# Sliding-window attention with a mixture of experts: values loaded twice per query block, one product per block and pair of heads

## The chip, the cores and the metric

The kernel runs on one core of a Trainium2 chip. Its engines are TensorE (PE, matrix products; PEld is its loading of weights), VectorE (DVE), ScalarE (ACT), GpSimd (POOL) and SyncE (SP, which here only issues DMAs). The metric is the device time of one execution in microseconds (us); the median of several runs counts.

## The reference

```
def _attn_ref(q, k, v):                       # 8 batches, 8 heads, 576 tokens, head size 64, float32
    scores = scale * np.matmul(q, k.transpose(0, 1, 3, 2))
    rel = pos[:, None] - pos[None, :]
    mask_plain = (rel >= 0) & (rel < 32)                          # heads 0 to 3
    mask_dil = (rel >= 0) & (rel < 32 * 4) & (rel % 4 == 0)       # heads 4 to 7
    scores = np.where(masks, scores, -1e9); attn = softmax(scores)
    return np.matmul(attn, v)

def _moe_ref(x, w_gate, w1, w2, capacity):    # x: 4608 x 512, 8 experts, capacity 80, hidden 1024
    probs = softmax(x @ w_gate); expert = argmax; gate_w = probs[expert]
    for e in range(8):
        tok = the (at most 80) tokens of expert e with the largest gate_w
        out[tok] = gate_w[tok] * (np.maximum(x[tok] @ w1[e], 0) @ w2[e])
    return out                                # rows of all other tokens are zero
```

## The kernel before

**Layout.** The dilated heads' tokens are permuted on the host, so that in both kinds of heads a block of 32 queries needs at most 64 keys: its own block of 32 and the block before it. `plan` puts four query blocks of 32 (one for each quarter of the 128 partitions) and both halves of the heads into one *tile*; there are 36 tiles, 4.5 for each of the 8 batches. In a tile `a` counts four pairs of heads (two plain, two dilated) and `u` the head within a pair. Keys (`k2`) and values (`v4`) of the two heads of a pair stand on alternate partitions, with zeros in the other head's place, so that one product serves both heads.

**A tile's chain** (`tile_chain`, L909): `scores` (L391) adds the mask through an identity product (L396, four of them) and multiplies queries and keys (L403, 16 products of 128 columns; each float32 product makes two rows in the trace). `smax` (L408) and `ssub` (L412) run on DVE, `sexp` (L418) on ACT. `ptrans` (L422) transposes the probabilities on PE, four products. `pcopy` (L428) brings them from PSUM into the tile `pts`: two copies of 64 partitions on ACT for one parity of key blocks, one of 64 partitions on DVE for the other. `pts` has a slot for a key block as a query block's own and one as the block before it; what isn't written stays zero from the start (L361). `pv` (L437) multiplies by the values: each value block of 64 keys stands in `v4` once, so a query block with an even number needs two products (its own block and the one before lie in different spans) and one with an odd number one product; a tile has mostly 24. `raw` (L459, ACT) copies the result out, `norm_r` (DVE) and `norm` (L469, POOL) divide by the sum, the row goes to DRAM (`xs`, L975), `xtrans` (L474) transposes it on PE, and `xcopy` (L498, ACT) puts pieces of it into `xT`.

**Gate and ranks.** For each batch `gate`, `fields`, `counts` and `merge` choose the 80 best tokens for each expert, in small steps on all engines beside the tiles. After the last tile they end in the list `irow` (L1048), from which `gather` (L284, an indirect DMA of POOL) fetches the tokens of the first expert.

**Experts.** Each expert has eight weight chunks of 512 KB (`wr`, `load_wc`, L166). `wsplit` (L181) splits one into a high part (`wh`, ACT, L191) and a low part (`wl`, DVE or POOL, L193), and `g1` and `g2` (L1079, L1111) run three products for each pair of parts. Of 64 chunks 11 are loaded during the tiles (L880, from tile 8 on every second tile), four at the last tile (L953), the rest when buffers come free.

**Order of work.** A planner (`drive`, L218) fixes the order of instructions on PE, DVE, ACT and POOL ahead of time from durations and penalties in the constants L32 to L41. Everything on the SP queue stands in the order of the calls: after tile i's scores a load of queries for tiles i+3 and i+4 (`after_scores`), after its row has gone out values (`after_norm`, L900) and every third time 512 KB of zeros for the output (`zero_out`, L386); the eight that are left go out after the last tile. A DMA on this queue waits until the one eight places ahead of it has landed. `warm` (L324) issues PE products whose results nobody reads: 40 at the start (`W0`), 15 at tile 2 (`W1`), 30 after the lists are ready (`W2`), and groups of eight between the last ranking steps (`NWA`, 88 in all).

Of the kernel before, what the change touches and what calls it, by code (L numbers as in the profile page):

```python
# [23 lines left out]
DIL = 4  # L24
# [11 lines left out]
d_sc, d_pv, d_ex = 1.25, 1.5, 0.55  # L36

l_pe, lat, LA, AGE = -0.011, 0.147, 5, 0.162
p_sc, p_pt, p_pv, p_xt, p_bg, e_bg, e_ct, e_mg, e_fl = -0.204, 0.096, 0.389, 0.407, 0.345, -0.051, 0.341, 0.278, 0.59
e_split, e_splitd, p_split, p_splitd, p_splitp, q_hi, q_lo, q_lop = 2.997, 0.642, 0.764, -0.636, 2.782, 1.204, 1.134, -1.508  # L40
q_ga, q_in, p_wa, q_h, q_hp, d_x, p_mg, p_fl = -2.51, 0.414, 0.723, 0.74, 0.248, 0.0, 0.332, 1.008  # L41


def plan(B, S):


    nb = S // 32
    lin = [(b, j) for b in range(B) for j in range(nb)]
    q = [[lin[4 * t:4 * t + 4], lin[4 * t:4 * t + 4]] for t in range(len(lin) // 4)]
    v = [[list(h) for h in t] for t in q]  # L50
    if B % 2 == 0 and nb == 18:
        o = [0, 9, 4, 13, 2, 1, 10, 5, 14, 11, 6, 15, 16, 7, 8, 3, 12, 17]
        w = [0, 1, 8, 9, 12, 13, 4, 5, 2, 3, 10, 11, 14, 15, 6, 7, 16, 17]
        b, t0 = B - 1, len(q) - 5
        for lst, od in ((q, o), (v, w)):
            seq = lst[t0][1][:2] + [(b, j) for j in od]
            for k in range(5):
                lst[t0 + k][1] = seq[4 * k:4 * k + 4]
    for t in q:

        t[1] = [t[1][i] for i in (1, 0, 3, 2)]
    return q, v
# [7 lines left out]
def build_consts(B, S, E, C):  # L70
    NC = -(-S // P)
    ncc = B * NC
    q, _ = plan(B, S)
    bf = ml_dtypes.bfloat16
    masks, sig, held = [], [], {}
    for halves in q:
        m = np.zeros((P, 2, 64), np.float32)
        for h in range(2):
            for n, (b, j) in enumerate(halves[h]):
                qi = 32 * j + np.arange(32)[:, None]  # L80

                ki = 32 * j + (np.arange(64) - 32 if j % 2 else np.arange(64) % 32 - 32 * (np.arange(64) // 32))[None, :]
# [37 lines left out]
def moe_attn_kernel(ctx: ExitStack, tc: tile.TileContext, io, dims, sig):  # L120
# [9 lines left out]
    KW = NG * S  # L130
    HB = S // 2
# [3 lines left out]
    qplan, vplan = plan(B, S)  # L135
    vpos = {}
    for t, halves in enumerate(vplan):
        for h in range(2):
            for i, bk in enumerate(halves[h]):
                assert bk[1] % 2 == i % 2  # L140
                vpos[h, bk] = (t, i // 2)
# [76 lines left out]
    def drive(chains, cost, done):  # L218
# [7 lines left out]
        while not done():  # L226
# [6 lines left out]
            for c in chains:  # L233
                ask = c[1]() if callable(c[1]) else c[1]
                if ask is not None:
                    eng, d, r = ask
                    s0 = max(clock[eng.split(".")[0]], r + l_pe * (eng[:2] == "PE"))
                    k = s0 + cost(c, eng, s0)
# [3 lines left out]
            _, end, c, eng, d = best  # L242
            clock[eng.split(".")[0]] = end
            advance(c, end)

# [14 lines left out]
    def split_lo(name):  # L260
# [5 lines left out]
        def ask():  # L266
            for (e, c, p, n), r in mine():
                return name, (0.00225 if pool_ else 0.00113) * 1024 / n + 0.03, r
# [25 lines left out]
    with ExitStack() as c2:  # L294
# [10 lines left out]
        NV = 3  # L305
# [29 lines left out]
        k2 = [qp.tile([P, 2, KW + HB], F32, name=f"k2_{i}") for i in range(2)]  # L335
# [4 lines left out]
        pts = [kp.tile([P, 2, 2, 2, 2, 2, 32], F32, name=f"pts_{i}") for i in range(2)]  # L340
# [7 lines left out]
        KS = (0, 64, 160, HB)  # L348
        kv = [k[:, :, 0:KW].rearrange("p u (a x) -> p u a x", a=2 * NG) for k in k2]
        nc.vector.memset(zero, 0.0)  # L350
        for u in range(2):
            nc.vector.memset(kv[0][:, u, :, 0:KS[1]], 0.0)
        for i in (1, 2):
            for u in range(2):
                (nc.vector, nc.gpsimd)[u].memset(kv[0][:, u, :, KS[i]:KS[i + 1]], 0.0)
# [4 lines left out]
        for i in range(2):  # L360
            nc.vector.memset(pts[i], 0.0)  # L361
        for u in range(2):
            nc.gpsimd.memset(k2[1][:, u, 0:KW], 0.0)
# [914 lines left out]
```

## Time and profile before

| | before |
|---|---|
| median of 3 runs | 327.98 us (325.33 to 331.28) |
| profiled execution, its own time | 326.13 us |
| its span, first to last instruction | 324.3 us |
| PE busy in the span | 291.6 us, 90% |
| DVE, ACT, POOL busy | 235.6, 196.7, 163.2 us |
| moved by DMA | 85.11 MB, 262 GB/s over the span |
| granted TensorE clock, mean | 0.974 of full speed |

The profile's page gives busy time by engine, the span in 40 slices (PEclk is the TensorE clock that was granted, in tenths), the chain of work that ended last, and the costliest groups of instructions with what ended the idle time before them. "issue" is time in which an engine waited for nothing that the profile shows. The stages are: up to 19 us the first loads; to 195 us the tiles; to 214 us the last ranks; from 216 us the experts; the span ends at 324.3 us.

### The profile page before, as it was taken

Reading aid. Unit: us, or ns where it says so; the run is one execution under the profiler, and the core shown is the slowest. Engines: PE = TensorE matmul, PEld = TensorE weight load, DVE = VectorE, ACT = ScalarE, POOL = GpSimd, SP = SyncE. Lnnn points to the kernel's source line nnn. Section 1 sums busy time; section 2 is a strip of 40 time slices with the busy share of each in tenths; the row PEclk is TensorE's granted clock in tenths of the full one; section 3 lists DMA queues with packets and bytes.
Section 4 is the critical chain, followed back from the end, with each engine's and each line's share of the span. In section 5 each row is a group of like instructions: output and inputs, shape, how many; then the busy total and the mean of one; then the engine's idle time right before and its main releaser. Section 6 shows DMA issues by size and latency. Waiting matters only on the chain.

```text
span 324.3 us, 11403 instructions
## 1 busy us (share of the span) xinstructions
PE 291.6 (90%) x4615; PEld 221.0 (68%) x4615; DVE 235.6 (73%) x636; ACT 196.7 (61%) x519; POOL 163.2 (50%) x208
## 2 busy tenths in 40 slices
PE   7669999999897999997999998778999999999992
PEld 6448788778776778766778875654566666666661
DVE  6327757969756868867879788785997887887550
ACT  6106567464743655762664763473889889889560
POOL 9302225356644833152333353359978878655522
PEclk9959999999999999999999999995999999999997
DMA  5973989949995889986734528977959999998000
GB/s 145 304 298 101 331 300 365 408 148 330 346 346 191 236 293 342 346 316 205 259 105 166 197 71 284 403 249 247 357 186 321 379 396 379 390 380 314 20 20 21
DMA packets 31396, 85.11 MB, mean 262 GB/s; under 512 B 5744, under 2 KB 7408, under 8 KB 30448
## 3 DMA queue, kind: packets, MB, share of 16 engines
q1 hardware_dynamic: 30064, 81.76, 70.9%
q0 software_dynamic: 1280, 2.62, 2.6%
q8 instruction: 36, 0.59, 0.8%
q14 instruction: 16, 0.13, 0.1%
HBM read 64.19 MB, written 20.19 MB: 260 GB/s over the span
## 4 chain that ended last, share of the span: by engine, by line
PE 50%; DMA 15%; DVE 14%; issue 8%; ACT 7%; POOL 3%; SPq 1%; POOLq 0%; ACTq 0%; DVEq 0%
PE pv L454 10%; PE sc L403 8%; PE hp L1087 7%; PE yps L1119 7%; PE xt L478 4%; PE pT L426 4%; DMA wr<-in_w 4%; DMA out<-zero 3%; DVE wl L193 3%; DMA k<-in_k 3%; PE sc L396 3%; DMA xs<-x 2%; DVE pts L434 2%; ACT wh L191 2%; ACT xT L503 2%
## 5 line engine op out<-in xcount | busy, mean ns | idle before, releaser
L193 DVE TENSOR_TENSOR wl<-wr,wh 128x1024 fp32r<-128x1024 f32 (+1 forms) x54 | 70.5, 1349 | 12.1 <-ACT wh L191 11.9
L471 POOL TENSOR_TENSOR x<-xr,rc 128x512 f32<-128x512 f32 x35 | 36.9, 1055 | 78.2 <-DVE rc L467 33.8
L191 ACT CAST wh<-wr 128x1024 fp32r<-128x1024 f32 (+1 forms) x72 | 64.0, 954 | 1.0 <-PE yps L1119 0.5
L454 PE MATMUL pv<-v,pts 128*32 128x130 f32 x1664 | 56.6, 274 | 4.1 <-issue 4.1
L454 PEld LDWEIGHTS pv<-v,pts 128*32 128x32 f32 x1664 | 47.0, 108 | 7.7 <-issue 7.0
L403 PE MATMUL sc<-k,q 128*32 128x128 f32 x1152 | 42.8, 289 | 6.2 <-DMA k<-in_k 3.5
L193 POOL TENSOR_TENSOR wl<-wr,wh 128x1024 fp32r<-128x1024 f32 (+1 forms) x18 | 41.0, 2282 | 14.4 <-PE yps L1119 7.5
L403 PEld LDWEIGHTS sc<-k,q 128*32 128x32 f32 x1152 | 35.5, 116 | 11.3 <-issue 8.1
L462 ACT COPY xr<-pv 128x520 f32<-128x520 f32 x35 | 20.7, 591 | 36.1 <-PE pv L454 35.3
L503 ACT COPY xT<-xt 128x64 f32<-128x64 f32 (+3 forms) x195 | 33.6, 312 | 13.1 <-PE xt L478 12.8
L434 DVE COPY pts<-pT 64x512 f32<-64x512 f32 x36 | 25.0, 694 | 19.3 <-ACT pts L432 18.8
L410 DVE TENSOR_REDUCE mx<-sc 128x8 f32<-128x512 f32 x36 | 24.6, 684 | 11.3 <-PE sc L403 10.8
L432 ACT COPY pts<-pT 64x256 f32<-64x256 f32 x72 | 23.7, 381 | 12.3 <-PE pT L426 12.2
L420 ACT ACTIVATE ex<-ex 128x512 f32<-128x512 f32 x36 | 23.0, 638 | 12.1 <-DVE ex L415 11.7
L415 DVE TENSOR_TENSOR ex<-sc,mx 128x512 f32<-128x512 f32 x36 | 24.8, 689 | 4.7 <-PE pT L426 3.8
L1087 PE MATMUL hp<-wh,xh 128*80 128x512 f32 x64 | 26.6, 416 | 0.4 <-ACT xh L1077 0.4
L287 POOL DMA_INDIRECT xg<-xs,irow x16 | 23.1, 1444 | 6.9 <-issue 3.4
L1087 PE MATMUL hp<-wl,xh 128*80 128x512 f32 x64 | 26.2, 410 | 0.2 <-DVE wl L193 0.2
L1087 PE MATMUL hp<-wh,xl 128*80 128x512 f32 x64 | 26.2, 409 | 0.0
L1119 PE MATMUL yps<-wh,hh 128*80 128x512 f32 x64 | 25.3, 395 | 0.0
L1119 PE MATMUL yps<-wh,hlo 128*80 128x512 f32 x64 | 25.2, 394 | 0.1
L1119 PE MATMUL yps<-wl,hh 128*80 128x512 f32 x64 | 25.0, 391 | 0.0
(137 smaller groups left out, 509.4 us busy)
## 6 DMA issues: line engine op xcount, KB each, us to landing
wr<-in_w SPq DMA_DIRECT2D x64, 512.0 KB, 7.6
v<-in_v SPq DMA_DIRECT2D x36, 260.0 KB, 4.2
xs<-x SPq DMA_DIRECT2D x36, 256.0 KB, 4.0
out<-zero SPq DMA_DIRECT2D x18, 512.0 KB, 6.6
q<-in_q SPq DMA_DIRECT2D x17, 512.0 KB, 6.9
k<-in_k SPq DMA_DIRECT2D x14, 576.0 KB, 6.2
q<-in_q SPq DMA_DIRECT2D x2, 256.0 KB, 3.0
k<-in_k SPq DMA_DIRECT2D x2, 256.0 KB, 7.8
```

The lines of the kernel that those rows point to most:

```text
L191: nc.scalar.copy(hi[:, s], w[:, s])
L193: eng.tensor_tensor(out=lo[:, s], in0=w[:, s], in1=hi[:, s].bitcast(F32), op=ALU.subtract)
L403: nc.tensor.matmul(out=ps[32 * j:32 * j + 32, a], lhsT=q[:, a // 2, a % 2, j, :], rhs=k2[b % 2][:, :, o:o + 2 * w].rearrange("p u (r y) -> ...
L410: nc.vector.tensor_reduce(out=st[t]["mx"], in_=st[t]["sc"].rearrange("p a u r k -> p (a u) (r k)"), axis=AX.X, op=ALU.max)
L415: nc.vector.tensor_tensor(out=st[t]["ex"].rearrange("p a k u -> p a u k"), in0=st[t].pop("sc").rearrange("p a u r k -> p a u (r k)"), in1= ...
L432: nc.scalar.copy(pts[t % 2][0:64, h, :, :, h], ps[0:64, h])
L434: nc.vector.tensor_copy(out=pts[t % 2][64:P].rearrange("p h g e s i q -> p (h g) (e s) i q")[:, :, 1:3], in_=ps[64:P].rearrange("p h g e i ...
L454: nc.tensor.matmul(out=ps[32 * j:32 * j + 32, h, 2 * g * (D + 1):2 * (g + 1) * (D + 1)].rearrange("p (u d) -> p u d", u=2), lhsT=pts[t % 2 ...
L471: eng.tensor_tensor(out=st[t]["x"].rearrange("p (h a) d -> p h a d", h=2), in0=st[t][of][:, :, :, 0:D], in1=st[t]["rc"].unsqueeze(3).broad ...
L503: copy(out=dst, in_=ps[:, HC * hh:HC * hh + HC, col:col + n])
L1087: nc.tensor.matmul(out=fs[e]["hp"][n][0:C], lhsT=a_[:, c, :], rhs=b_[:, sl], start=(c == 0 and q == 0), stop=(c == NKC - 1 and q == 2))
L1119: nc.tensor.matmul(out=fs[e]["y"][0:C], lhsT=a_[:, f, :], rhs=b_[:, sl], start=(f == 0 and q == 0), stop=(f == NFC - 1 and q == 2))
```

## The change

The values' layout in DRAM now holds, for each query block, the 64 keys from the block before it to its own end, so every value stands there twice. `load_v` loads one tile at a time, 2 x 260 KB, into four buffers (`NV`; before: two tiles at a time into three). `pv` is one product for each query block and pair of heads, 16 in a tile, with no accumulation. `pcopy` is one copy of all 128 partitions into a tile from a pool, on ACT or DVE, as the planner finds (`either`): 23 on ACT and 13 on DVE. `pts` isn't zeroed any more. Keys have a row of their own for each pair of heads with 32 zeros ahead, and are loaded in three pieces of 128, 192 and 256 keys. The dilated blocks of a tile aren't swapped, so a tile's `xT` is copied in fewer pieces (116 on ACT; before 195 on ACT and two on DVE). The first queries go through ACT's queue. Zeros go out after every sixth tile, and 13 of the 18 after the last. The four weight chunks of the last tile are requested behind its row. The planner's constants are others; it adds a price where PE goes from products of 32 columns to whole ones. `W2` is 64 and `NWA` is 0.

```diff
-ZR, ZI, IW, W0, W1, W2, XC, SP0 = 2, 6, 8, 40, 15, 30, 1, 2
-FB, CB, TE, NWA, XC0 = 3, 6, 34, 8, 2
-CUTS = (2,)
+ZR, ZI, IW, W0, W1, W2, XC, SP0 = 2, 6, 8, 40, 15, 64, 1, 2
+FB, CB, TE, NWA, XC0 = 0, 1, 35, 0, 2
+CUTS = (3,)
...
-        NV = 3
+        NV = 4
...
+        for t in range(2):
+            nc.scalar.dma_start(q2[0][:, t:t + 1], io["q"][0, :, t:t + 1])
+        KS = (0, P, 2 * P + 64, S)
...
-        for i in range(2):
-            nc.vector.memset(pts[i], 0.0)
...
+        def load_v(t):
             for u in range(2):
-                nc.sync.dma_start(v4[p % NV][u::2, u], io["v"][p, u])
+                nc.sync.dma_start(v4[t % NV][u::2, u], io["v"][t, u])
...
-        def pcopy(t, half):
-            ps = st[t]["pT"].rearrange("p (h g) i e q -> p h g e i q", h=2)
-            if half == 0:
-                for h in range(2):
-                    nc.scalar.copy(pts[t % 2][0:64, h, :, :, h], ps[0:64, h])
-            else:
-                nc.vector.tensor_copy(out=pts[t % 2][64:P].rearrange("p h g e s i q -> p (h g) (e s) i q")[:, :, 1:3],
-                                      in_=ps[64:P].rearrange("p h g e i q -> p (h g) e i q"))
+        def pcopy(t, copy):
+            st[t]["pt"] = sp.tile([P, NG, P], F32, tag="pts", name=f"pts_{t}")
+            copy(out=st[t]["pt"], in_=st[t].pop("pT"))
...
         def pv(t):
...
-                    cols = [(0, k)] + [(1, k - 1)] * (k % 2 == 0 and 32 * k % (S if h == 0 else S // DIL) > 0)
...
+            for a in range(NG):
+                h, g = a // 2, a % 2
                 for j in range(4):
+                    nc.tensor.matmul(out=ps[32 * j:32 * j + 32, h, 2 * g * (D + 1):2 * (g + 1) * (D + 1)].rearrange("p (u d) -> p u d", u=2),
+                                     lhsT=st[t]["pt"][:, a, 32 * j:32 * j + 32], rhs=v4[t % NV][:, :, j, h, g, :],
+                                     start=True, stop=True, skip_group_check=True)
...
         def after_norm(i):
-            if i % 2 == 0 and 2 < (i + 2) // 2 < NT // 2:
-                load_v((i + 2) // 2)
-            if ZI <= i < NT and i % 3 == 0:
+            if NV <= i + 2 < NT:
+                load_v(i + 2)
+            if ZI <= i < NT and i % 6 == 0:
                 zero_out(zeros.pop(0))
```

Three places show how the order moves. On PE, from the scores of the sixth tile to the end of its neighbours' products (sc scores, pv the product with the values, pT transposed probabilities, xt transposed rows), before:

```order
L403 MATMUL sc_475<-k_1_143,q_0_144 32x128 x16
L454 MATMUL pv_503<-v_1_147,pts_149 32x130 x4
L454 MATMUL pv_503<-v_0_146,pts_149 32x130 x2
L454 MATMUL pv_503<-v_1_147,pts_149 32x130 x6
L454 MATMUL pv_503<-v_0_146,pts_149 32x130 x2
L454 MATMUL pv_503<-v_1_147,pts_149 32x130 x10
L478 MATMUL xt_534<-c_ident,x_470 128x128 x4
L426 MATMUL pT_548<-c_ident,ex_448 128x128 x4
```

and from the same scores in the change:

```order
L403 MATMUL sc_487<-k_1_143,q_0_144 32x128 x16
L462 MATMUL xt_516<-c_ident,x_443 128x128 x4
L426 MATMUL pT_531<-c_ident,ex_463 128x128 x4
L438 MATMUL pv_536<-v_3_149,pts_482 32x130 x16
L398 LDWEIGHTS c_identb
```

The 24 products that read two buffers of values have become 16 that read one, and they stand next to the following tile's scores. On SP, the first requests of the program, before:

```order
L375 DMA q_0_144<-in_q 128x512
L372 DMA k_0_142<-in_k 64x8x64 x2
L856 DMA c_identb<-in_identb 128x128
L382 DMA c_mask<-in_mask 128x256
L375 DMA q_0_144<-in_q 128x512
L372 DMA k_0_142<-in_k 64x8x96 x2
L861 DMA c_ident<-in_ident 128x128
L379 DMA v_0_146<-in_v 64x1040 x2
L375 DMA q_1_145<-in_q 128x1024
L382 DMA c_mask<-in_mask 128x1408
L372 DMA k_0_142<-in_k 64x8x128 x2
L379 DMA v_1_147<-in_v 64x1040 x2
```

and in the change, where both requests for q_0 stand on ACT's queue:

```order
L374 DMA k_0_142<-in_k 64x4x128 x2
L839 DMA c_identb<-in_identb 128x128
L384 DMA c_mask<-in_mask 128x256
L374 DMA k_0_142<-in_k 64x4x192 x2
L384 DMA c_mask<-in_mask 128x256
L844 DMA c_ident<-in_ident 128x128
L374 DMA k_0_142<-in_k 64x4x256 x2
L377 DMA q_1_145<-in_q 128x512
L381 DMA v_0_146<-in_v 64x1040 x2
L381 DMA v_1_147<-in_v 64x1040 x2
L377 DMA q_1_145<-in_q 128x512
L384 DMA c_mask<-in_mask 128x1152
```

The third piece of the first keys now stands ahead of the values and of the second pair of queries. On SP, the last rows (xs), the weight chunks (wr) and the zeros around the last tile, before:

```order
L975 DMA xs<-x_3813 128x512
L975 DMA xs<-x_3902 128x512
L169 DMA wr_3_4017<-in_w 128x1024
L172 DMA wr_4_4019<-in_w 128x1024
L172 DMA wr_5_4021<-in_w 128x1024
L172 DMA wr_6_4023<-in_w 128x1024
L975 DMA xs<-x_4025 128x512
L975 DMA xs<-x_4034 128x512
L387 DMA out<-zero 128x2x512 x8
L172 DMA wr_7_4446<-in_w 128x1024
```

and in the change:

```order
L960 DMA xs<-x_3594 128x512
L960 DMA xs<-x_3661 128x512
L960 DMA xs<-x_3700 128x512
L157 DMA wr_3_3704<-in_w 128x1024
L160 DMA wr_4_3706<-in_w 128x1024
L160 DMA wr_5_3708<-in_w 128x1024
L160 DMA wr_6_3710<-in_w 128x1024
L389 DMA out<-zero 128x2x512 x13
L160 DMA wr_7_3747<-in_w 128x1024
```

The chunks have moved behind the last two rows, and 13 blocks of zeros stand between them and the next chunk.

## Rows read from the trace of the kernel before

**Rows 1.** The page, busy time of each engine, its share of the span, instructions:

```profile
PE 291.6 (90%) x4615; PEld 221.0 (68%) x4615; DVE 235.6 (73%) x636; ACT 196.7 (61%) x519; POOL 163.2 (50%) x208
```

**Rows 2.** Busy time by window: the tiles, the last ranks, the first experts:

```profile
core 0: us, PE busy (x) PEld busy (x) DVE busy (x) ACT busy (x) POOL busy (x), PEclk, DMA share, GB/s
20.00:195.00 175.00, 163.24 (x3757) 133.92 (x3749) 131.28 (x453) 102.10 (x375) 72.57 (x134) 0.99 0.73 255
197.00:214.00 17.00, 13.12 (x200) 10.45 (x200) 13.40 (x79) 7.98 (x23) 5.58 (x17) 1.00 1.00 366
216.00:246.00 30.00, 27.11 (x122) 16.60 (x123) 25.41 (x28) 20.49 (x31) 26.04 (x16) 0.89 0.78 259
```

**Rows 3.** The chain of work that ended last, in tiles (start us, us, what):

```profile
30.70 0.87 PE sc L403 x32
...
48.94 1.47 PE pv L454 x48
```

**Rows 4.** The page's groups (busy us, mean ns of one, idle before and releaser):

```profile
L454 PE MATMUL pv<-v,pts 128*32 128x130 f32 x1664 | 56.6, 274 | 4.1 <-issue 4.1
L503 ACT COPY xT<-xt 128x64 f32<-128x64 f32 (+3 forms) x195 | 33.6, 312 | 13.1 <-PE xt L478 12.8
L434 DVE COPY pts<-pT 64x512 f32<-64x512 f32 x36 | 25.0, 694 | 19.3 <-ACT pts L432 18.8
L432 ACT COPY pts<-pT 64x256 f32<-64x256 f32 x72 | 23.7, 381 | 12.3 <-PE pT L426 12.2
```

**Rows 5.** PE's longest waits between 20 and 195 us (total, times, longest):

```profile
PE pv L454 <- issue: 4.1, 5, 1.9
PE sc L403 <- issue: 2.7, 3, 1.8
```

**Rows 6.** The page's DMA issues (count, KB each, median us to landing):

```profile
wr<-in_w SPq DMA_DIRECT2D x64, 512.0 KB, 7.6
v<-in_v SPq DMA_DIRECT2D x36, 260.0 KB, 4.2
xs<-x SPq DMA_DIRECT2D x36, 256.0 KB, 4.0
out<-zero SPq DMA_DIRECT2D x18, 512.0 KB, 6.6
q<-in_q SPq DMA_DIRECT2D x17, 512.0 KB, 6.9
k<-in_k SPq DMA_DIRECT2D x14, 576.0 KB, 6.2
```

**Rows 7.** Further windows, columns as in the group of windows above, in which the DMA engines were full:

```profile
76.00:96.00 20.00, 18.52 (x439) 15.14 (x437) 14.59 (x47) 11.95 (x45) 13.15 (x27) 1.00 1.00 350
52.00:64.00 12.00, 11.43 (x273) 9.34 (x269) 9.34 (x35) 6.17 (x23) 5.48 (x13) 1.00 1.02 401
48.00:52.00 4.00, 4.00 (x99) 3.42 (x99) 3.63 (x14) 3.07 (x12) 0.91 (x2) 1.00 1.03 324
```

**Rows 8.** The chain at the start of the program, third and fourth tile's scores:

```profile
10.07 8.59 DMA k<-in_k
18.79 1.92 PE sc L403 x28
...
22.31 1.71 PE sc L403 x32
```

**Rows 9.** The page's DMA rate in 40 slices of 8.1 us:

```profile
GB/s 145 304 298 101 331 300 365 408 148 330 346 346 191 236 293 342 346 316 205 259 105 166 197 71 284 403 249 247 357 186 321 379 396 379 390 380 314 20 20 21
```

**Rows 10.** Timeline from the lists to the first expert (start us, us, instructions, idle before):

```profile
213.23 1.83 PE L330 MATMUL warm<-ones 128*128 128x128 bf16 x30
213.41 0.18 DVE L1048 TENSOR_REDUCE irow<-tail 80x16 int32<-80x32 f32 x1 [0.75 <-PE tail L822]
...
213.88 1.17 POOL L287 DMA_INDIRECT xg<-xs,irow  x1 [3.26 <-DMA out<-zero]
...
216.65 0.36 PE L1070 MATMUL tx<-c_ident,xg 80*128 80x80 f32 x2 [1.59 <-DMA xg<-xs,irow]
```

More of the change, by code (lines that the diff above doesn't have):

```diff
@@ L242, in drive, with change, either, ask @@
             _, end, c, eng, d = best
+            if eng[:2] == "PE":
+                mode["PE"] = MODES.get(eng)
             clock[eng.split(".")[0]] = end
             advance(c, end)
+    mode = {"PE": None}
+    def change(eng):
+        return d_ch if eng in MODES and mode["PE"] != MODES[eng] else 0.0
+    def either(r, *of):
+        def ask():
+            eng, d = min(of, key=lambda x: max(clock[x[0]], r) + x[1])
+            ask.eng = eng
+            return eng, d, r
+        return ask
     hiq = [(0, c, p, SP0) for c in range(8) for p in range(SP0)]
@@ L451, in pv @@
-            for n in range(max(len(w) for w in work)):
+            for a in range(NG):
+                h, g = a // 2, a % 2
                 for j in range(4):
-                    for h, g, s, vb, vc, first, last in work[j][n:n + 1]:
-                        nc.tensor.matmul(out=ps[32 * j:32 * j + 32, h, 2 * g * (D + 1):2 * (g + 1) * (D + 1)].rearrange("p (u d) -> p u d", u=2),
-                                         lhsT=pts[t % 2][:, h, g, j % 2, s if h == 0 else 1 - s, j // 2, :], rhs=v4[vb][:, :, vc, h, g, :],
-                                         start=first, stop=last, skip_group_check=True)
+                    nc.tensor.matmul(out=ps[32 * j:32 * j + 32, h, 2 * g * (D + 1):2 * (g + 1) * (D + 1)].rearrange("p (u d) -> p u d", u=2),
+                                     lhsT=st[t]["pt"][:, a, 32 * j:32 * j + 32], rhs=v4[t % NV][:, :, j, h, g, :],
+                                     start=True, stop=True, skip_group_check=True)
@@ L923, in tile_chain @@
                 yield None
-            e = yield "DVE", 0.72, e
+            e = yield "DVE", 0.68, e
             ssub(t)
@@ L937, in tile_chain @@
                 yield None
-            ea = yield "ACT", 0.56, e + lat
-            pcopy(t, 0)
-            e = yield "DVE", 0.68, e + lat
-            pcopy(t, 1)
-            ev["pt", t] = e = max(e, ea)
+            ask = either(e + lat, ("ACT", 0.58), ("DVE", 0.7))
+            ev["pt", t] = e = yield ask
+            pcopy(t, nc.vector.tensor_copy if ask.eng == "DVE" else nc.scalar.copy)
             while t >= 1 and ("x0", t - 1) not in ev:
@@ L975, in tile_chain @@
             nc.sync.dma_start(xs[t * P:(t + 1) * P, :], st[t]["x"].rearrange("p h d -> p (h d)"))
+            if t == NT - 1:
+                for e_, c in chunks[NW:NW + N3]:
+                    load_wc(e_, c, wx["w3"])
             after_norm(t + 2)
@@ L985, in tile_chain @@
                     yield from until(("xTfree", (b - 2, 0)))
-            if t < NT - 2:
-                e = yield "ACT", sum(act(2 * p[-1]) for p in pcs), e + lat
-                for p in pcs:
-                    xcopy(t, *p, nc.scalar.copy)
-            else:
-                ea, p0, p1 = e + lat, [p for p in pcs if p[0] == 0], [p for p in pcs if p[0]]
-                e = yield "ACT", sum(act(2 * p[-1]) for p in p1), ea
-                for p in p1:
-                    xcopy(t, *p, nc.scalar.copy)
-                e = max(e, (yield "DVE", sum(dve(2 * p[-1]) for p in p0), ea))
-                for p in p0:
-                    xcopy(t, *p, nc.vector.tensor_copy)
-            ev["xT", t] = e
+            ask = either(e + lat, ("ACT", 0.05 + sum(0.06 + 0.00083 * 2 * p[-1] for p in pcs)), ("DVE", 0.06 + sum(0.07 + 0.00104 * 2 * p[-1] for p in pcs)))
+            e = yield ask
+            for p in pcs:
+                xcopy(t, *p, nc.scalar.copy if ask.eng == "ACT" else nc.vector.tensor_copy)
+            ev["xT", t] = e + 0.1
         def each(f):
```

183 lines of the change are left out of this document (80 added, 103 removed).

## Prediction

> **What bounds the kernel now.** Busy shares come first: PE is busy 90% of the span, DVE 73%, ACT 61% [rows 1]. By stage it is clearer: from 20 to 195 us, the tiles, PE is busy 163.2 of 175 us, DVE 131, ACT 102, and the DMA engines 73% [rows 2]. 34 tiles run there (the third starts at 18.79 us [rows 8]), 5.18 us for each. PE sets their pace: of the 11.8 us that it idles, 6.8 are "issue" in the middle of the score and value products [rows 5], and only some 5 are waits for others. From 216 us PE runs the experts nearly without a gap (27.1 of 30 us [rows 2]). Between, from 197 to 214 us, the ranks are a chain of small steps that all engines wait for. So an instruction fewer on PE in a tile is worth its time, if the inputs keep up; one fewer on ACT or DVE is worth little by itself.
>
> **The change, part by part.** *Value products.* The trace has 1664 of them [rows 4], two for each float32 product; 16 a tile make 16 x 2 x 36 = 1152, so 512 go. A full tile's 48 take 1.47 us [rows 3], 30.6 ns each: 512 x 30.6 = **-15.7 us**. By the price of a score product (0.87 / 32 = 27.2 ns [rows 3]) it is 13.9. I take the row of the thing itself. It is worth nothing where something else than PE sets the pace (rivals).
>
> *Copies of probabilities.* 72 on ACT (23.7 us) and 36 on DVE (25.0, with 18.8 us of waiting for ACT ahead of them [rows 4]) become 23 on ACT and 13 on DVE. A whole copy moves the same 512 columns as the DVE copy does, so 0.69 us bounds it above, and two of ACT's halves, 0.76, come to about the same. That is some 16 us less on either engine, and 79 fewer pieces of xT (33.6 us for 195 [rows 4]) take a few more from ACT. All of it lies beside PE, so it is priced at a part of the 5 us that PE waits for others: **-1**, between 0 and -3.5. If PE were no longer the pace, these engines would have room: DVE would stand at about 115 of 160 us.
>
> *Start.* Tile 2 (the third) waits 8.6 us for the third piece of the keys [rows 8]. By the shapes in the order, 3.28 MB were requested up to that piece; now 2.20 MB are requested up to the last input of the same scores, which is half a pair of queries behind it. The difference, 1.09 MB at some 300 GB/s [rows 9], is 3.6 us. But tile 3's queries now stand behind the first two loads of values: 3.52 MB, 0.24 MB more than stood ahead of the keys, so they land about 0.8 us after 18.8, at 19.6; these scores ran at 22.31 [rows 8]. The gain that stays is the smaller, **-2.7**. Zero is the bound above if the queue is slower. Below, -5: after that wait the third tile's scores ran at the lower granted clock (1.92 us for 28 rows against 0.87 for 32 [rows 3, 8]), and a shorter wait may keep the higher one.
>
> *DMA in the tiles.* A tile asked for 0.27 MB each of values, queries, keys and its own row, 0.17 of zeros and, from tile 8 to 28, 0.26 of weights [rows 6]: 1.49 MB. Now the values are 0.53 and the zeros 0.09, together 1.67 MB. The products bring the pace to 5.18 - 15.7/34 = 4.72 us, so the demand is 354 GB/s. With the engines full they moved 350 GB/s for 20 us, 401 for 12 us and, at worst, 324 for 4 us [rows 7]. At 350 a tile takes 4.77 us, 1 us in 20 tiles; at 324 it takes 5.15, 8.6 us; at 401 nothing. Values are requested four tiles ahead and queries three, some 14 us against a landing time of 4.2 to 6.9 us [rows 6], which covers the first 5 us or so of falling behind. I take **+2**, between 0 and +9. A row xs that lands later delays nobody until three tiles on.
>
> The Trainium skill, in "DMA: Bandwidth & Descriptors", section "Bandwidth", puts the memory's share for one core at about 358 GB/s when both cores of a pair stream, and lets a single one reach 425. By the lower figure a tile's 1.67 MB would take 4.66 us (an estimate from that page), just inside PE's pace; the trace's 401 GB/s over 12 us [rows 7] lies above it, so here the measurement decides.
>
> *Last ranks.* The 88 `warm` products between the steps go. They kept the clock at full level: 1.00 with PE busy 13.1 of 17 us [rows 2], of which 88 x 61 ns (1.83 us for 30 [rows 10]) = 5.4 were theirs. At the lower level the other 7.7 us could at most double, if all stood on the chain; the second part of the last batch, in turn, has two chunks of tokens where it had three. I take **+1.5**, between -1 and +7. The rows xs no longer stand behind 2 MB of weights, which is worth nothing as long as the lists come later than the rows.
>
> *First expert.* Queued behind the ranks are now 64 warm products (3.9 us at 61 ns, 7.8 at the lower level). The first gathered half came 3.2 us after `irow` [rows 10], so PE may reach it 0.5 to 4.4 us late; but before, PE idled there and ran the first expert below full clock (0.89 over 30 us [rows 2]). The five further blocks of zeros (2.6 MB) are still being written when the gather starts, so its two halves may take some us longer. The later weight chunks stand behind these zeros, 6.6 us at 400 GB/s. What hides that is the DMA engines' spare time to 246 us, (1 - 0.78) x 30 = 6.6 us [rows 2]: just enough. I take **+1** for all of this, between -2 and +8.
>
> **Sum.** 326.1 (the profiled execution's own time) - 15.7 - 1 - 2.7 + 2 + 1.5 + 1 = 311.2; I predict **311 us**. That execution lies 0.6% below the median of 327.98, so seen from the median the change is -5.2%.
>
> **Rivals.** *The DMA engines become the pace of the tiles.* For it: a demand of 354 GB/s on average, loads that come in bursts because SP waits for each row, and full windows as low as 324. Against it: 401 GB/s for 12 us. At 324 without the cover of the prefetch the term is +9 in place of +2, 318, and with loads that come in bursts up to 322 us.
>
> *Slower: the mix with doubled values can't be moved faster than the loads of the start.* Values go to 64 partitions in 260 KB pieces, and a slice of the start, full of such loads, shows about 300 GB/s [rows 9]. At 270 a tile takes 6.18 us; 20 such tiles cost (6.18 - 5.18) x 20 = 20 us more than before, against 14 x 0.46 = 6.4 saved in the others, 3.7 by start and copies, and +2.5 at the end: 326.1 + 20 - 6.4 - 3.7 + 2.5 = 338.5. It decides at about 300 GB/s: there a tile takes 5.57 us and the sum is 326.3, no change; over 2% slower it becomes below 285.
>
> *No change: PE's rows overlap anyway.* A row lasts 274 ns [rows 4] and one starts every 30.6, so many run beside each other, and fewer rows might not shorten the stream. Against it: the price is that of a whole tile's stream, not of a row, and 32 score rows take 0.87 us where 48 value rows take 1.47 [rows 3]. Then only start and end are left, -2.7 - 1 + 2 + 1.5 + 1 = +0.8: 327.
>
> *Better.* The clock stays up at the start and the gaps shrink with the work on ACT and DVE: -5 and -3.5 in place of -2.7 and -1, and no DMA cost: 304.5.
>
> In the Trainium skill, "Runtime: NRT & Kernel Launch", section "Instruction fetch mechanics", says that instructions come by DMA in blocks of 256 and that crossing a block is mostly hidden. No row here names the cause of the 6.8 us of "issue" [rows 5]; if it is that, 1024 fewer PE instructions, four blocks, would save 6.8 x 4 / 36 = 0.8 us (9230 PE instructions [rows 1] are 36 such blocks), and the sum would be 310.4.
>
> **Numbers.** The forecast (304 to 317) has 0.53, DMA pace (318 to 322) 0.18, slower 0.13, no change 0.08, better 0.08. To leave out no more than 2 in 10 the range goes from 303 to 327. The forecast's own range is 304 to 317. A measurement of this kernel tells about 2% from no change. Faster by over 2% (under 321) are forecast, better and half of the DMA case: 0.70; the other half and no change are within 2%: 0.17; slower 0.13.
>
> **What would show it.** After: 1152 value products at about 0.9 to 1.0 us a tile and a pace near 4.7 us; third tile's scores near 15 us; DMA share near 0.9 in the tiles, with rows of PE that wait for queries or values if the DMA rival is right; granted clock and length from the last row to `irow` (17 us before) for the ranks; the time from `irow` to the first expert's products. A pace of 5 us or more, or more than before's 108 us from 216 us to the end, would make the prediction wrong.

## The result and the profile after

The change made the kernel faster: 310.48 us (median of 4 runs, 307.84 to 312.47) against 326.65 us before on the same chip (323.89 to 331.28), a ratio of 0.9505 with an interval of 0.937 to 0.9639. The profiled execution has a span of 306.0 us, 18.3 less than before's.

By stage, from the starts and ends of rows in both traces (us):

| stage | before | after | difference |
|---|---|---|---|
| to the third tile's scores (before: to their fifth row, behind the keys) | 18.79 | 13.28 | -5.5 |
| from there to the end of the last value product | 175.3 | 159.1 | -16.2 |
| from there to `irow` | 19.3 | 21.1 | +1.7 |
| from `irow` to the end | 110.9 | 112.5 | +1.6 |

The page of the kernel after: busy time by engine (as [rows 1]), and the DMA rate in 40 slices of 7.65 us (as [rows 9]).

```profile
PE 268.0 (88%) x4060; PEld 205.1 (67%) x4060; DVE 233.0 (76%) x616; ACT 190.5 (62%) x401; POOL 148.5 (49%) x169
...
GB/s 167 279 366 400 396 375 406 408 407 400 409 339 342 349 334 329 352 325 403 274 210 110 71 251 402 403 372 369 335 260 381 400 335 378 373 324 266 24 21 21
```

PE lost 23.6 us of work, and its share fell: it waits more than before. The windows view shows for what (columns as in [rows 2]); first before, from 20 to 160 us, in which both kernels run tiles:

```profile
20.00:160.00 140.00, 129.45 (x2993) 106.20 (x2989) 102.59 (x348) 80.17 (x295) 59.75 (x110) 0.99 0.81 284
```

and after, the same stretch and a part of it:

```profile
20.00:160.00 140.00, 124.92 (x2862) 104.50 (x2858) 102.70 (x382) 82.58 (x215) 48.35 (x82) 0.99 0.98 360
40.00:80.00 40.00, 35.74 (x848) 30.16 (x839) 28.45 (x112) 23.71 (x61) 15.11 (x28) 0.99 1.03 404
```

The DMA engines went from 81% to 98% and moved 404 GB/s for 40 us. PE idled 15.1 us instead of 10.6. Its longest waits in this stretch, after (as [rows 5]):

```profile
PE pv L438 <- issue: 6.2, 6, 1.4
PE sc L403 <- DMA q<-in_q: 2.5, 2, 1.9
PE sc L403 <- issue: 1.8, 2, 1.3
PE pT L426 <- issue: 1.2, 2, 0.9
PE csp L690 <- issue: 1.1, 1, 1.1
PE msa L755 <- issue: 1.0, 1, 1.0
PE lt L536 <- issue: 0.9, 1, 0.9
```

Only 2.7 us are waits for queries and values. 12.2 us are "issue" (6.8 before). Four such waits in a row in PE's timeline:

```profile
98.81 0.64 PE L438 MATMUL pv<-v,pts 128*32 128x130 f32 x14 [1.41 <-issue]
...
105.38 1.07 PE L438 MATMUL pv<-v,pts 128*32 128x130 f32 x26 [1.42 <-issue]
...
111.95 0.38 PE L755 MATMUL msa<-c_identb,oh 128*128 128x128 bf16 x2 [1.03 <-issue]
...
118.62 0.30 PE L403 MATMUL sc<-k,q 128*32 128x128 f32 x2 [0.44 <-issue]
```

They fall in the middle of products whose inputs are there, 6.6 us apart. The windows between them, with PE alone, count the rows:

```profile
98.80:105.37 6.57, 5.16 (x127) 1.00 1.00 365
105.37:111.94 6.57, 5.54 (x125) 1.00 0.97 314
111.94:118.61 6.67, 6.22 (x125) 1.00 0.99 347
```

Each has 125 to 127 products and as many loads of weights; with PE's semaphore instructions, which the trace holds too, that makes 255 to 257 instructions. All 13 "issue" waits of the stretch stand at such a distance, or a multiple of it, from each other. The page's DMA queues have a line for instructions:

```profile
q8 instruction: 32, 0.52, 0.7%
```

32 packets of 16 KB, and PE has 2 x 4060 instructions, 31.7 times 256 (36 packets and 9230 instructions before). The trace also has the time of each packet. One of them starts at 102.91 us and lands at 103.87; the DMA view of 102.9 to 103.9 us holds it:

```profile
q8 instruction: 1, 0.02, 6.0%
```

PE goes on 1.51 us later, at 105.38. So it is at each of the 13 waits: PE goes on 1.2 to 1.6 us after the landing of such a packet. So "issue" here is PE at the end of a block of 256 instructions whose successor comes late. The same holds for the eight waits of this kind before (6.8 us): 255 to 257 instructions apart, or a multiple, and each ends 1.3 to 1.6 us after a packet. The packets take about 1 us in any case; what differs is when they start. From 20 to 160 us of the change that is on average 3.5 us after PE has crossed the border before; from 159 to 172 us, where the DMA engines have room (a share of 0.30 from 160 us on), it is 0.5 to 0.7 us.

The groups that answer to [rows 4], after (line, operation, count | busy, mean ns | idle before):

```profile
L438 PE MATMUL pv<-v,pts 128*32 128x130 f32 x1152 | 42.2, 279 | 6.7 <-issue 6.2 <-ACT pts L430 0.3 <-DMA v<-in_v 0.2
...
L487 ACT COPY xT<-xt 128x256 f32<-128x256 f32 (+5 forms) x116 | 34.0, 404 | 10.4 <-PE xt L462 10.1
...
L430 ACT COPY pts<-pT 128x512 f32<-128x512 f32 x23 | 13.7, 596 | 7.4 <-PE pT L426 7.4
L430 DVE COPY pts<-pT 128x512 f32<-128x512 f32 x13 | 8.8, 677 | 2.8 <-PE pT L426 2.8
```

1152 value products as announced; a tile's 32 take 0.89 us in the chain. The copies of probabilities took 48.7 us on ACT and DVE before and 22.5 after. The pieces of xT are fewer but larger and cost ACT as much as before (33.6 and 34.0 us).

### The profile page after: what moved, and what is told of

The parts are those of the page before. It is cut to its first block, busy times and chain, and to the rows that moved or that the text cites. A ratio compares the mean times of both kernels' runs of the same rounds, so it can differ in the third digit from the quotient of the medians.

```text
span 306.0 us, 10182 instructions
## 1 busy us (share of the span) xinstructions
PE 268.0 (88%) x4060; PEld 205.1 (67%) x4060; DVE 233.0 (76%) x616; ACT 190.5 (62%) x401; POOL 148.5 (49%) x169
## 4 chain that ended last, share of the span: by engine, by line
PE 54%; DMA 17%; issue 12%; DVE 12%; POOL 2%; ACT 1%; POOLq 0%; SPq 0%; DVEq 0%; ACTq 0%
PE yps L1099 9%; PE pv L438 9%; PE hp L1067 8%; PE sc L403 8%; DMA v<-in_v 6%; DMA q<-in_q 5%; PE pT L426 4%; PE xt L462 4%; DMA xg<-xs,irow 3%; PE sc L398 2%; DMA out<-yo,itok 2%; PE lt L536 2%; PE KLp L647 2%; DVE wl L181 2%; DMA wr<-in_w 2%
## 5 line engine op out<-in xcount | busy, mean ns | idle before, releaser
L181 DVE TENSOR_TENSOR wl<-wr,wh 128x1024 fp32r<-128x1024 f32 (+1 forms) x51 | 80.0, 1623 | 4.3 <-ACT wh L179 3.3
L179 ACT CAST wh<-wr 128x1024 fp32r<-128x1024 f32 (+1 forms) x72 | 65.8, 958 | 5.0 <-PE yps L1099 3.8
L181 POOL TENSOR_TENSOR wl<-wr,wh 128x1024 fp32r<-128x1024 f32 (+1 forms) x21 | 45.7, 2180 | 9.1 <-ACT wh L179 6.1
L438 PE MATMUL pv<-v,pts 128*32 128x130 f32 x1152 | 42.2, 279 | 6.7 <-issue 6.2
L403 PE MATMUL sc<-k,q 128*32 128x128 f32 x1152 | 40.6, 279 | 5.5 <-DMA q<-in_q 3.5
L403 PEld LDWEIGHTS sc<-k,q 128*32 128x32 f32 x1152 | 33.7, 112 | 11.0 <-DMA q<-in_q 5.5
L487 ACT COPY xT<-xt 128x256 f32<-128x256 f32 (+5 forms) x116 | 34.0, 404 | 10.4 <-PE xt L462 10.1
L438 PEld LDWEIGHTS pv<-v,pts 128*32 128x32 f32 x1152 | 33.4, 110 | 9.7 <-issue 8.5
L293 POOL DMA_INDIRECT xg<-xs,irow x16 | 24.3, 1522 | 10.8 <-DVE lstf L1030 5.5
L1067 PE MATMUL hp<-wh,xh 128*80 128x512 f32 x64 | 25.7, 402 | 0.4 <-ACT xh L1057 0.4
L426 PE MATMUL pT<-c_ident,ex 128*128 128x128 f32 x144 | 23.8, 286 | 2.2 <-issue 1.2
L462 PE MATMUL xt<-c_ident,x 128*128 128x128 f32 x144 | 22.8, 282 | 0.7 <-POOL x L455 0.7
```

Of the source, the lines that this page charges most:

```text
L179: nc.scalar.copy(hi[:, s], w[:, s])
L181: eng.tensor_tensor(out=lo[:, s], in0=w[:, s], in1=hi[:, s].bitcast(F32), op=ALU.subtract)
L293: nc.gpsimd.indirect_dma_start(out=xg[:, h * HD:(h + 1) * HD], out_offset=None, in_=xrows, in_offset=bass.IndirectOffsetOnAxis(ap=irow.bit ...
L403: nc.tensor.matmul(out=ps[32 * j:32 * j + 32, a], lhsT=q[:, a // 2, a % 2, j, :], rhs=k2[b % 2][:, :, a, 32 * k:32 * k + 64], start=False, ...
L426: nc.tensor.transpose(out=st[t]["pT"][:, a], in_=ex[:, a].rearrange("p k u -> p (k u)"), identity=ident)
L438: nc.tensor.matmul(out=ps[32 * j:32 * j + 32, h, 2 * g * (D + 1):2 * (g + 1) * (D + 1)].rearrange("p (u d) -> p u d", u=2), lhsT=st[t]["pt ...
```

## The experiments

Each kernel is compared with the kernel before by the ratio of runs on one chip; the difference to the change's own ratio, 0.9505, times 328 us, gives "against the change", with the two half intervals added as squares. Spans are those of the profiled executions (306.0 us for the change).

| kernel | ratio to before (interval) | against the change, us | span |
|---|---|---|---|
| 24 value products | 0.9879 (0.9729 to 1.0029) | +12.3 +- 6.6 | 322.4 |
| values loaded once | 0.9082 (0.8968 to 0.9196) | -13.9 +- 5.8 | 291.1 |
| half of the values | 0.9235 (0.9136 to 0.9334) | -8.9 +- 5.5 | 298.9 |
| both engines copy | 0.9695 (0.9589 to 0.9801) | +6.2 +- 5.6 | 311.7 |
| keys behind the values | 0.9602 (0.9541 to 0.9663) | +3.2 +- 4.8 | 311.9 |
| warm products in the ranks | 0.9735 (0.9635 to 0.9836) | +7.5 +- 5.5 | 315.3 |
| 30 warm products | 0.9553 (0.9486 to 0.9621) | +1.6 +- 4.9 | 307.4 |
| zeros every third tile | 0.9388 (0.9277 to 0.9499) | -3.8 +- 5.7 | 304.5 |
| zeros in the idle stretch | 0.9493 (0.9391 to 0.9595) | -0.4 +- 5.5 | 305.1 |
| weights at tiles 28 to 35 | 0.9408 (0.93 to 0.9516) | -3.2 +- 5.7 | 305.7 |
| weights at tiles 24 to 35 | 0.9407 (0.9346 to 0.9468) | -3.2 +- 4.8 | 304.6 |
| before, 16 value products | 0.9639 (0.954 to 0.9738) | (against before: -11.8 +- 3.2) | 314.9 |

**24 value products.**

```diff
+                    for _ in range(2 - j % 2):
-                    nc.tensor.matmul(out=ps[32 * j:32 * j + 32, ...
+                        nc.tensor.matmul(out=ps[32 * j:32 * j + 32, ...
```

> The change with 24 value products a tile in place of 16: in the query blocks of even number the same product is issued twice into the same place, all other work and the order of all engines are the same. 8 x 2 x 36 = 576 more rows on PE. If PE sets the pace of the tiles, the time grows by 576 x 27 to 31 ns = 15.5 to 17.6 us, to 326 to 328 us, and the rows of a tile take 1.3 to 1.5 us instead of 0.9. If the DMA engines already set it in the first half (they are full from 20 to 140 us of the profile after), the rows there cost nothing and only the tiles behind 130 us pay: about 10 tiles x 0.44 = +4 to +6 us.

12 us more by the ratio, 16.4 by the spans. A row of PE's timeline shows that the added rows were dearer than meant:

```profile
112.51 1.97 PE L439 MATMUL pv<-v,pts 128*32 128x130 f32 x48
```

About 1.9 us for 48 rows, 40 ns each, where the same number took 1.47 before [rows 3]. Here a product and its copy follow each other into the same 32 partitions of PSUM; before, the products went round the four blocks. That this is the reason is not shown. So PE got 29.3 us of work (297.3 us busy on the page for 268.0), 0.8 a tile, and the pace from the tenth to the thirtieth tile grew only from 4.64 to 5.09 us. About half of the added work fell into time that PE had spent waiting: its "issue" waits from 20 to 160 us went from 12.2 to 2.1 us, in this window:

```profile
20.00:160.00 140.00, 136.19 (x3074) 119.62 (x3074) 92.49 (x344) 75.90 (x195) 44.48 (x76) 1.00 0.96 343
```

PE still paces the tiles, but not alone.

**Values loaded once.**

```diff
-            if NV <= i + 2 < NT:
-                load_v(i + 2)
```

> The change without the loads of values from tile 4 on (the four buffers keep the first four tiles' values), so that a tile asks for 0.53 MB less; the products run on what is there, so the output differs. If the doubled values cost little (the prediction's +2 us in the tiles), the time falls by 1 to 4 us, mostly by PE's waits for queries and values between 13 and 40 us; PE's gaps named issue (12 us between 20 and 160 us) stay. Rival: the DMA engines pace the tiles of the change, and the gaps named issue, which have doubled against before, are instructions that come late behind full DMA queues: then the pace falls from 4.5 us to 4.1 or less, the issue gaps shrink to under 6 us and the time falls by 8 to 15 us.

The rival's figure: 14 us less, pace 4.09 us. The window and the longest waits from 20 to 160 us:

```profile
20.00:160.00 140.00, 134.06 (x3135) 113.95 (x3138) 116.43 (x442) 93.91 (x256) 56.65 (x96) 1.00 0.72 249
```

```profile
PE sc L403 <- DMA q<-in_q: 1.8, 2, 0.9
PE sc L403 <- issue: 1.5, 3, 0.8
```

The same order on PE, 273 more of its products within 140 us, and "issue" is down to 2.1 us. The loads do hold the tiles up, by late instructions more than by late data. My first theory (1 to 4 us, "issue" stays) falls.

**Half of the values.**

```diff
-                load_v(i + 2)
+                nc.sync.dma_start(v4[(i + 2) % NV][0::2, 0], io["v"][i + 2, 0])
```

> The change with one of the two loads of values from tile 4 on left out (260 KB a tile less, so a tile asks for what it asked for before; the output differs). The loads of values as a whole cost 13 to 14 us (the run without them). If the price is that of a queue near its limit (the gaps named issue, each at the border of a block of instructions, come back only when the DMA engines are full), most of it is gone with half of the bytes: 9 to 13 us less than the change, a pace of 4.1 to 4.25 us, issue under 5 us between 20 and 160 us. If each byte costs the same, 6 to 7 us less and 4.35 us. By the prediction's own term (+2 us for the doubling) it would be 2 us less.

9 us less: the doubling of the loads, which this run takes back in bytes, costs about that; the interval begins at 3.4 and leaves the predicted 2 us out. The pace is 4.50 us from the tenth to the thirtieth tile, "issue" 7.2 us and the waits for queries 0.2 us. The first half of the bytes gives 9 of 14 us by the ratios, and 7.1 of 14.9 by the spans. That is no more than the same price for each byte, within these intervals; that the price rises towards the limit, as I expected, is not shown.

**Before, 16 value products.**

```diff
-                    cols = [(0, k)] + [(1, k - 1)] * (k % 2 == 0 and 32 * k % (S if h == 0 else S // DIL) > 0)
+                    cols = [(0, k)]
```

> The kernel before with the second products of the even query blocks left out (the product with the block before is missing there, so the output differs): 512 rows fewer, all loads, copies and the order of work as before. By the prediction's price, 30.6 ns a row, the time falls by 15.7 us, and by 13.9 at the price of a score row. If a row that is left gets cheaper too, a tile's value products take 0.9 us in place of 1.47 and it falls by 18 to 20. If PE's rows overlap anyway, by under 3. Against all of these the issue gaps may grow from 6.8 us by 2 to 4, since a tile's loads then come within less time.

The tiles in the windows view, before and then with the rows left out; both windows end at the last value product:

```profile
20.00:194.00 174.00, 162.73 (x3753) 133.50 (x3745) 130.42 (x449) 102.10 (x375) 72.05 (x134) 0.99 0.73 257
```

```profile
20.00:184.00 164.00, 147.57 (x3229) 117.85 (x3227) 129.30 (x448) 100.88 (x375) 71.69 (x134) 0.99 0.76 272
```

PE's busy time falls by 15.2 us, the predicted 15.7; the stretch by 10, the whole by 11.8 (9.4 by the spans). Within that stretch PE waits 16.4 us for 11.3, although "issue" is down to 2.1 us up to 160 us: the new waits are for the small steps and copies of DVE and ACT, and one of 1.9 us for queries. (I had expected that the "issue" waits would grow by 2 to 4 us.) Some of the new waits:

```profile
PE msa L771 <- DVE oh L598: 2.2, 5, 0.7
PE csp L706 <- DVE gtl L697: 2.0, 7, 0.4
PE sc L396 <- DVE ex L415: 1.9, 4, 0.7
...
PE pT L426 <- DVE pts L434: 1.1, 2, 0.6
```

So fewer rows alone are not worth their price while the two engines copy as before.

**Both engines copy.**

```diff
-            copy(out=st[t]["pt"], in_=st[t].pop("pT"))
+            copy(out=st[t]["pt"], in_=st[t]["pT"])
+            other = nc.scalar.copy if copy == nc.vector.tensor_copy else nc.vector.tensor_copy
+            other(out=sp.tile([P, NG, P], F32, tag="spare", ...), in_=st[t].pop("pT"))
```

> The change with each tile's probabilities copied by both engines, by the second one into a tile that nobody reads: ACT and DVE each copy as much as before (some 0.6 us more a tile on one of them), the products and loads are as in the change. By the prediction (copies lie beside PE, worth 1 us, 3.5 at most) the time grows by 0 to 3.5 us. If DVE, which is busy 76% of the span after, has become a second pace, it grows by more than 6 us and PE's waits for ACT and DVE, now near nothing in the tiles, reach that.

6 us more, about the threshold that I had named for a second pace; the interval reaches down to 0.6 us. The added copies, in the lines view:

```profile
L432 DVE COPY spare<-pT 128x512 f32<-128x512 f32 x23 | 15.9, 690 | 11.0 <-ACT pts L430 10.9
...
L432 ACT COPY spare<-pT 128x512 f32<-128x512 f32 x13 | 7.8, 598 | 5.5 <-DVE pts L430 5.4
```

The thirtieth tile starts 1.3 us later than in the change, the last value product ends 6.4 us later: it is lost in the last six tiles, where the gates and ranks of DVE stand beside them. PE waits 2.6 us there for DVE and ACT (0.3 in the change) and 2.6 for "issue" (1.7), and the same 797 products take it 2.2 us longer, at a granted clock of 0.88 behind 165 us (1.00 in the change). No single wait carries it, and a part of the 6 us is the clock.

**Keys behind the values.**

```diff
-        load_k(0, KS[2], KS[3])
         load_q(1, slice(0, 1))
         load_v(0)
         load_v(1)
         load_q(1, slice(1, 2))
+        load_k(0, KS[2], KS[3])
```

> The change with the third piece of the first keys requested behind the first two tiles' values and the second pair of queries, as before the change; nothing else moves. The third tile's scores, at 13.3 us in the change, then run at about 17 to 19 us. If that wait is paid in full, as the prediction has it, the end comes 2.7 to 4 us later. If the loads that follow set the pace up to 40 us (PE waits for queries at 17.3 and 20.8 us and for values at 38.5), the wait only takes their place: the tenth tile starts within 1 us of the change's 42.4 us and the time stays within 1 us.

The loads in front keep the keys back; the third tile's scores stop after four rows and go on at the lower clock:

```profile
16.76 1.92 PE L403 MATMUL sc<-k,q 128*32 128x128 f32 x28 [2.25 <-DMA k<-in_k]
```

28 rows in 1.92 us, as before [rows 8]. The fourth tile's scores start 4.5 us later (21.8 for 17.3), the tenth tile 1.9 us, and the time is 3.2 us longer. That fits the predicted 2.7, but its interval holds zero too, so it is not settled.

**Warm products in the ranks.**

```diff
-FB, CB, TE, NWA, XC0 = 0, 1, 35, 0, 2
+FB, CB, TE, NWA, XC0 = 0, 1, 35, 8, 2
```

> The change with the groups of eight warm products between the last ranking steps put back, everything else as it is. The clock in the ranks was 0.56 between 180 and 200 us without them. If the lower clock lies on the chain of the ranks, the way from the last value product to irow (21 us after) shortens by 2 to 4 us, and the whole by as much at most. If the steps of the other engines hide it, it stays at 20 to 21 us, and the time within 1 us.

Neither: the way from the last value product to `irow` grew from 21.1 to 25.7 us. The ranks' windows, before and after:

```profile
196.00:213.40 17.40, 13.52 (x197) 10.30 (x194) 13.84 (x78) 7.75 (x23) 5.47 (x16) 1.00 1.01 366
```

```profile
176.00:193.30 17.30, 10.32 (x97) 7.07 (x92) 11.44 (x63) 9.67 (x27) 5.42 (x16) 0.53 0.91 335
```

and one row of this run's timeline:

```profile
192.94 5.18 PE L336 MATMUL warm<-ones 128*128 128x128 bf16 x48
```

The two windows were cut to the same length; they don't show what the clock costs. PE's steps do lie on the chain that ends in `irow`. In the change they are 7.4 of its last 17.7 us; three rows of the chain view:

```profile
180.85 0.84 PE KLp L647 x3
181.69 0.84 PE lt L542 x8
...
182.93 1.04 PE lt L557 x4
```

What the lower clock costs can be read where the same steps ran at another one: from DVE's normalisation of the last tile to `irow` it takes 17.7 us in the change at a granted clock of 0.54, and 17.2 in two other runs at 0.62 and 0.63 ("weights at tiles 24 to 35", "24 value products"). With the warm products it takes 22.3 us. They bring the clock back only for short stretches (0.64 on average from 176 to 200 us), the 48 of the row above take 108 ns each on average instead of 61 [rows 10], and the next step stands behind them. To take them out was a gain in this order of work.

**30 warm products.**

```diff
-ZR, ZI, IW, W0, W1, W2, XC, SP0 = 2, 6, 8, 40, 15, 64, 1, 2
+ZR, ZI, IW, W0, W1, W2, XC, SP0 = 2, 6, 8, 40, 15, 30, 1, 2
```

> The change with 30 warm products behind the lists, as before, in place of 64. PE then waits some 4 us longer for the first gathered half (7.5 us behind irow either way). If the 64 hold the clock up for the first expert, the clock falls to about 0.7 for the first 10 us of the experts and the end comes 2 to 3.5 us later (before, the way from the first expert's first product to the end was 107.65 us, after 105.0). If they don't matter, the time stays within 1 us.

PE waits longer and starts at the lower clock, for 3 us (before, the clock fell after four products, for 7 us):

```profile
202.03 0.53 PE L1050 MATMUL tx<-c_ident,xg 80*128 80x80 f32 x2 [4.11 <-DMA xg<-xs,irow]
202.94 0.71 PE L1067 MATMUL hp<-wh,xh 128*80 128x512 f32 x1 [0.38 <-ACT xh L1057]
...
206.22 0.40 PE L1067 MATMUL hp<-wh,xl 128*80 128x512 f32 x1
```

The change's first products take 0.39 to 0.46 us. 1.6 us more by the ratio, 1.4 by the spans: not distinguishable from nothing.

**Zeros every third tile; zeros in the idle stretch.**

```diff
-            if ZI <= i < NT and i % 6 == 0:
+            if ZI <= i < NT and i % 3 == 0:
```

> The change with a block of zeros after every third tile, as before: eight blocks instead of 13 stand behind the last tile. If these blocks make the first gather slow (7.5 us from irow to the first expert's products, 3.2 before), that time falls to 3.5 to 5 us and the 64 warm products then end last; the end comes 2 to 3 us earlier. Against it 2.6 MB more are written while the DMA engines are full up to 130 us: if these set the tiles' pace there, up to 2.6 MB / 390 GB/s = 6.7 us are given back, and the time grows by up to 4 us.

```diff
-            if ZI <= i < NT and i % 6 == 0:
+            if ZI <= i < NT - 6 and i % 6 == 0:
+                zero_out(zeros.pop(0))
+            if NT - 6 <= i <= NT:
+                zero_out(zeros.pop(0))
```

> The change with 14 of the blocks of zeros sent two at a time after the rows of the last tiles (from 130 us on, where the DMA engines have room), none behind the last row. If the zeros hold up the first gather, the way from irow to the first expert's products falls from 7.5 us to 5.5 or so (the 64 warm products take 5.8 us behind irow and then end last), and the end comes 2 us earlier or more, since the weight chunks behind the zeros are requested earlier. If it is the next weight chunks that it shares the DMA engines with, it stays at 7 us and the time within 1 us.

Neither is told from the change. From `irow` to the first gathered half's transposes it takes 7.5 us in the change, 6.5 with eight blocks behind the last tile and 6.0 with none. With none, the warm products end last (PE's timeline):

```profile
193.71 6.37 PE L336 MATMUL warm<-ones 128*128 128x128 bf16 x64
199.92 0.31 PE L1053 MATMUL tx<-c_ident,xg 80*128 80x80 f32 x2
```

So in these traces zeros hold the gather up by 1 to 1.5 us, and no more can be had while the 64 products stand there.

**Weights later.**

```diff
+        early = chunks[:NW]
...
-            if IW <= i and i % 2 == 0 and (i - IW) // 2 < NW:
-                c = (i - IW) // 2
-                load_wc(c // 8, c % 8)
+            for _ in range({28: 1, 30: 1, 31: 1, 32: 2, 33: 2, 34: 2, 35: 2}.get(i, 0)):
+                load_wc(*early.pop(0))
```

> The change with the eleven weight chunks that are loaded during the tiles requested at tiles 28 to 35 in place of every second tile from the eighth on: 5 MB less up to 125 us, where the DMA engines are full; the order of the other engines is the same and the first split of a chunk comes at 162 us as before. If full DMA engines hold the tiles up (leaving out 8.7 MB of values took 9 us), moving 5 MB out of that stretch takes 3 to 6 us off the change, to 305 to 307 us, and the issue gaps between 20 and 160 us fall from 12 to under 8 us. If only the values' own loads matter, or if the chunks now come late for the splits beside the ranks, it is 309 to 313 us.

and with one chunk each at tiles 24, 26, 28, 30, 32, 33 and 34 and four at tile 35:

> The change with the eleven weight chunks requested at tiles 24, 26, 28, 30, 32, 33 and 34, one each, and four at tile 35: most of them still leave the full stretch up to 125 us, but the tiles 31 to 34 aren't given two each. If it is fullness of the DMA engines that counts and not the order of the loads, the pace stays at 4.5 us to the last tile, its scores run at 157 to 159 us (161.9 in the change, 159.8 with the chunks at tiles 28 to 35), and the time is 304 to 307 us, the fastest of all. If the gain given back there comes from something else, it is 308 to 311 us.

The thirtieth tile starts 4 us earlier in both (131.0 and 131.2 for 135.2 us), as expected, and the last scores only 2.9 us earlier in both. The "issue" waits from 20 to 160 us are 8.9 and 10.8 us, where I had expected under 8. The window of the second:

```profile
20.00:160.00 140.00, 127.46 (x2934) 106.66 (x2934) 105.29 (x394) 85.26 (x224) 49.11 (x83) 0.99 0.97 346
```

More is done by 160 us than in the change, at nearly the same DMA share. Both medians are near 308.5 us, 2 us under the change's; the intervals overlap, so that they beat it is not shown. Why the last six tiles give a third back stayed open.

## Why the prediction was right, point by point

| term | predicted, us | found, us | from |
|---|---|---|---|
| value products | -15.7 | -15.2 of PE's work, -11.8 of time alone | before with 16 |
| copies' relief | -1 (0 to -3.5) | -6.2 +- 5.6 | both engines copy |
| start | -2.7 (0 to -5) | -3.2 +- 4.8 for the keys | keys behind the values |
| DMA in the tiles | +2 (0 to +9) | +8.9 +- 5.5 | half of the values |
| last ranks | +1.5 (-1 to +7) | +1.7 | stages of the two traces |
| first expert | +1 (-2 to +8) | +1.6 | stages of the two traces |

The found terms add up to -9 or -12 us, the measured change is -16.2 by the ratio and -18.3 by the spans. The runs' terms need not add up to the whole, since PE's waits for one thing hide those for another: products and copies give 12 and 6 us apart, and the traces' tiles lost 16.2 us with the loads' price already in it.

**What held.** PE sets the pace, and the rows taken from it are worth their price in its work; "no change as rows overlap" is refuted. The tiles' pace is 4.64 us (4.7 said), the value products take 0.89 us (0.9 to 1.0 said), the third tile's scores run at 13.3 (near 15 said). The way from the first expert's first transposes to the end is 105.0 us, under before's 107.65; against that the way from `irow` to them grew from 3.2 to 7.5 us, which together is the term's +1.6. PE did not reach them late because of the 64 warm products: it waited 1.96 us for the gathered rows behind these. The DMA share in the tiles, 0.98, is above the "near 0.9" said.

One reading of the start was wrong without harm: the 8.6 us of [rows 8] are the load's time in the chain. PE itself had run four rows of the third tile's scores at 15.85 us and then stood 2.5 us. The term was priced by bytes and not by these 8.6 us.

**Mis-sized: the DMA term.** The demand of 354 GB/s was right (360 moved), but I compared it with a limit, as if nothing were lost below that. The loss comes earlier, at the borders of PE's instruction blocks, which the sum did not contain. I had seen 6.8 us of "issue" in [rows 5] and left its cause open, with a gain of 0.8 us if it were instruction blocks. It is these, as the packets show in both traces, and it grew to 12.2 us instead. The Trainium skill, in "Runtime: NRT & Kernel Launch", section "Instruction fetch mechanics", gives blocks of 256 instructions, which the trace confirms (255 to 257 instructions between waits), and says that crossing one is mostly hidden. That holds with values loaded once (2.1 us); in the change it does not. Fullness of the DMA engines alone doesn't decide it: with 24 value products their share is 0.96 and "issue" 2.1 us. There the packets start 2.9 us after the border (3.5 in the change), and PE's own work in a block is 5.6 us (5.5). Why so little decides it stayed open.

**Mis-sized: the copies.** I priced them against the 5 us that PE waited for others before. But once PE's rows are fewer, ACT and DVE would have been late (5 us of new waits with 16 products before): the relief must be priced against the faster kernel. The two errors, +7 and -5, nearly cancel in the sum; that 311 came so near to 310.5 is luck to that extent.

**Right for another reason: the ranks.** The clock fell as feared, to 0.53, but the 1.7 us are not its price. They stand ahead of the chain: DVE begins the last tile's normalisation 3.4 us after the last value product, 0.8 before, because steps of the ranks stand in front of it in its order. From there to `irow` it takes 17.7 us at the lower clock and 18.5 before, where the steps came in another order and warm products stood among them. The warm products would have cost 4.6 us.

**The rivals.** "The DMA engines become the pace" describes what happened in mechanism (98% full, 9 us) better than my +2, but not in time, because the copies were worth more. "Slower" needed loads under 300 GB/s; they ran at 346 to 404 in the full stretches.

## What to carry to other kernels

Price what a change takes from a second engine against the kernel as it will be after it, not against the waits of the kernel before. Where PE waits for "issue" in the middle of a product, count the instructions between two such waits: at a fixed distance it is the instruction stream (compare when the packets of the instruction queue land), and loads that come near the DMA engines' limit can make it longer before any data is late. Warm products in the middle of a chain of small steps can cost more than the clock that they are to hold.

## What the runs showed of the hardware

- PE's gaps at borders of 256 instructions are up to 1.4 us each in the change, 12.2 us from 20 to 160 us; 2.6 us was the longest ("keys behind the values"). PE goes on 1.2 to 1.6 us after an instruction packet has landed, at all of these and at the eight of the kernel before.
- The DMA engines moved 404 GB/s for 40 us in this mix of 128- and 64-partition loads, writes of rows and zeros. The Trainium skill's figure for one core of a pair that both stream, 358 GB/s ("DMA: Bandwidth & Descriptors", section "Bandwidth"), was not the limit here.
- 48 value rows take 1.47 us when successive products go to different blocks of 32 partitions [rows 3], and about 1.9 us when each product of an even place is issued twice in a row into the same one: 31 and 40 ns a row.
- The same chain of small steps on all engines, from the last normalisation to `irow`, took 17.7 us at a granted clock of 0.54 and 17.2 us at 0.62.
